# Attention and routing in front of a mixture of experts: logits from products of their own, and token reads carried into the routing

## The chip, the core and the metric

The kernel runs on one core of a Trainium2 chip. The metric is the device time of one execution in microseconds; of several runs the median is given. Engines are called TensorE (PE in the profile, its weight loads PEld), VectorE (DVE), ScalarE (ACT), GpSimd (POOL) and SyncE (SP, which only issues transfers here).

## What is computed

Cross attention between 512 tokens and 32 states for 8 batches and 8 heads of 64, in both directions; then all 576 rows of a batch go through a gate and one of 8 experts.

```
scores = 0.125 * x @ state.T;  a = softmax(scores);  xread = a @ state
scores2 = 0.125 * state @ x.T; a2 = softmax(scores2); sread = a2 @ x
x = concat([xread, sread], rows)            # 8 batches x 576 rows x 512
logits = x @ w_gate;  local = sigmoid(x @ w_local)
expert of row s: argmax(logits) if s == 0 or local < 0.5, else that of row s-1
out = softmax(logits)[expert] * (relu(x @ w1[expert]) @ w2[expert])
```

The choice of expert runs along the rows of a batch, so routing needs the logits of every row of the batch.

## The kernel before

The work has three stages: attention over eight batches, routing, experts. The tile framework is told to keep the order in which the program issues instructions (`manual_schedule`), so every engine's queue is the order of the calls in `Attention.run`, written out by hand: a loop over batches with three of them in flight, `now`, `then` and `later`.

One batch goes like this. `scores` multiplies states by tokens on TensorE: two banks of 128 x 512, one for each half `u` of the heads, partitions holding 4 heads x 32 states. From them:

- over tokens: maximum (`nb`, L387), exponential with its sum (`e2`, `z2`, L399), `turn` (four TensorE transposes each half, L445), a copy to SBUF (`turned_to`, L448), `state_reads` (L458), `states_to` (scaling by 1/z2, L464), a store to `rows` (L473).
- over states: a 32x32 block transpose on VectorE (`turned`, L410) brings tokens to the partitions, `over_states` takes the maximum over 32 states on VectorE (L417) and subtracts it on GpSimd (L418), `exponents` on ScalarE (L422), `shares` sums on VectorE (L426), adds 1e-9 (L427), inverts (L428) and multiplies on GpSimd (L429); `turn_back` (L435) turns the blocks back to `a`.

`token_reads(c)` then makes the result for 128 tokens: for each half one product of `a` with `sd`, which is 265 columns wide, 256 of states (block diagonal over heads) and 9 of states times gate weights. So the 9 logits (8 experts and the local gate) come out beside the values. The 530 columns are copied from PSUM (L485): by VectorE for c = 1 of all batches but the last, by ScalarE otherwise. GpSimd adds the two halves' 9 columns to `lt` (L507); for the last tokens VectorE does it straight from PSUM (L489, L490). One transfer stores 512 tokens of values to `rows` (L508). Logits of the states' rows come from `rt` (L470) by four small products (L500) and a copy (L502).

`rows` is a table in device memory from which the experts gather their tokens.

`Routing.route` is one chain. `choose` turns logits into an expert or "as before" (seven batches ahead of the last one, then the last). The choices are transposed on TensorE (`seq`, L611), a scan on VectorE runs along the rows (L620), products bring it back (`back`, L624), comparison gives `oh`, two products count (`tot`, `pre`, L637 and L638), and small VectorE and ScalarE steps make the first place of every expert, then a place for every row. `slots.expert` (L691) lets SyncE load the first weights; `two` (L763) lets GpSimd gather the first tokens. In gaps TensorE runs products whose result nobody reads (`keep`, L600): nine, five, twenty and eight of them.

The experts use nearly all of SBUF for weights; memory of attention and of the experts is opened one after the other. GpSimd clears `sd` and `lt` at the start. Attention uses 8 PSUM banks: two for scores, two shared (`t`), and two pairs for reads.

Of the kernel before, what the change touches and what calls it, by code (L numbers as in the profile page):

```python
# [50 lines left out]
def kernel(  # L51
# [31 lines left out]
    def banks(ctx, n):  # L83
        ps = ctx.enter_context(tc.tile_pool(name="ps", bufs=n, space=PSUM))
        return lambda parts=P, n=512, dt=F32: ps.tile([parts, n], dt, tag="ps", name="ps")

# [6 lines left out]
    lt = keep.tile([P, B, NC, E + 1], F32, name="lt")  # L93

# [5 lines left out]
    with ExitStack() as phase:  # L100
        make_identity(nc, ident)
        start = Attention(phase, tc, xn, xt, st, stt, wgl, wgs, lt, rows)
        route.constants(ident)
        nc.gpsimd.memset(lt, 0.0)
        start.diagonal(range(2))
        nc.gpsimd.memset(none, 0.0)
        nc.sync.dma_start(out=rows[NT:].rearrange("o q x -> o (q x)"), in_=none)
        start.run(route)
    with ExitStack() as phase:
        bank = banks(phase, 6)  # L110

        sums = phase.enter_context(tc.tile_pool(name="sums", bufs=1, space=PSUM))
        sums = [sums.tile([P, 512], F32, name=f"sum{i}") for i in range(2)]
        experts(phase, tc, bank, sums, w1, w2, rows, slots, route, route.route(bank, sums, lt, slots), out)
# [21 lines left out]
A = G * SC * 4  # L136


class Attention:


    def __init__(self, ctx, tc, xn, xt, st, stt, wgl, wgs, lt, rows):
        nc = self.nc = tc.nc
        self.xn, self.xt, self.lt, self.rows = xn, xt, lt, rows
        self.wg, self.wh = wgs[:, 0], wgs[:, 1]
        once = ctx.enter_context(tc.tile_pool(name="once", bufs=1))
        self.xp = ctx.enter_context(tc.tile_pool(name="xp", bufs=3))
        self.wk = ctx.enter_context(tc.tile_pool(name="wk", bufs=2))
        self.tp = ctx.enter_context(tc.tile_pool(name="tp", bufs=2))
        self.sm = ctx.enter_context(tc.tile_pool(name="sm", bufs=4))  # L150
        self.ps = ctx.enter_context(tc.tile_pool(name="aps", bufs=1, space=PSUM))
        self.vps = ctx.enter_context(tc.tile_pool(name="vps", bufs=2, space=PSUM))

# [5 lines left out]
        self.x_t = {0: self.load_t(0)}  # L159
# [4 lines left out]
        self.x_t[1] = self.load_t(1)  # L164
        self.x_n = {0: self.load_n(0)}


        self.sd = once.tile([P, B, G * VW], F32, name="sd")
        nc.gpsimd.memset(self.sd, 0.0)
# [7 lines left out]
    def diagonal(self, ks):  # L177
        nc = self.nc
        for k in ks:
            r = slice(32 * k, 32 * k + 32)  # L180
            to = self.sd[r, :, E + 1:E + 1 + D].rearrange("p b (g d) -> p b g d", g=G)
            nc.scalar.copy(to[:, :, :, DH * k:DH * k + DH],
                           self.states_of[r].rearrange("p (b g d) -> p b g d", b=B, g=G))

    def load_t(self, b):
        nc = self.nc
        xs = []
        for i in range(2):
            x_t = self.xp.tile([P, KT // 2, S], F32, name=f"x_t{i}")
            nc.sync.dma_start(out=x_t.rearrange("p k s -> p (k s)"), in_=self.xt[b][:, i * D * 2:(i + 1) * D * 2])  # L190
            xs.append(x_t)
        return xs

    def load_n(self, b):
        x_n = self.xp.tile([P, SC, G, KT, DH], F32, name="x_n")
        self.nc.sync.dma_start(out=x_n.rearrange("p c u k d -> p (c u k d)"), in_=self.xn[b])
        return x_n
# [4 lines left out]
    def bank(self, name, parts=P):  # L202
        return self.ps.tile([parts, 512], F32, name=name)

    def gates(self):
        nc = self.nc
        ws = [self.bank(f"t{u}") for u in range(G)]
        for u, w in enumerate(ws):
            r = slice(64 * u, 64 * u + 64)
            for b in range(B):  # L210
                for k in range(KT):
                    nc.tensor.matmul(w[32 * k:32 * k + 32, b * (E + 1):(b + 1) * (E + 1)],
                                     lhsT=self.states(b)[r, k, :], rhs=self.wh[r, k, :], start=True, stop=True)
        for u, w in enumerate(ws):
            nc.scalar.copy(self.sd[:, :, u * (E + 1 + D):u * D + (u + 1) * (E + 1)],
                           w[:, :B * (E + 1)].rearrange("p (b e) -> p b e", b=B))

    def keep(self, n):

        for i in range(n):  # L220
            self.nc.tensor.matmul(self.idle[:, 0, :], lhsT=self.zero[:, :P], rhs=self.zero, start=True, stop=True)

    def run(self, route):

        self.ident = route.ident
        self.idle = self.vps.tile([P, G, 512], F32, name="v")
        self.keep(10)
        now, then = Batch(self, 0), Batch(self, 1)
        now.scores()
        for b in (2, 3):  # L230
            self.x_t[b], self.x_n[b - 1] = self.load_t(b), self.load_n(b - 1)

        for u in range(G):
            now.turned(u)
            now.over_states(u)
        now.maximum(0)
        now.scaled(0)
        now.exponents(0)
        self.gates()
        now.exponents(1)  # L240
        now.exponents_over_tokens(0)
        now.shares(0)
        now.maximum(1)
        now.scaled(1, self.nc.vector)
        now.exponents_over_tokens(1)
        now.shares(1)
        self.keep(6)
        now.turn(0)
        self.diagonal([2, 3])
        then.scores()  # L250
        now.turn(1)
        now.turn_back(0)
        now.turn_back(1)
        for u in range(G):
            then.turned(u)
            then.over_states(u)
        now.token_reads(0)
        now.turned_to(0)
        now.turned_to(1)
        now.state_reads()  # L260

        later = Batch(self, 2)
        self.load(0)
        then.maxima()
        then.exponents(0)
        then.exponents(1)
        then.exponents_over_tokens(0)
        then.shares(0)
        then.exponents_over_tokens(1)
        then.shares(1)  # L270
        now.invert()
        now.token_reads(1)
        now.states_to()
        now.token_reads(2)
        now.states_to_rows()
        later.scores()
        then.invert()
        later.maxima()
        then.turn(0)
        then.turned_to(0)  # L280
        then.turn(1)
        now.token_reads(3)
        then.turned_to(1)
        then.turn_back()
        later.exponents_over_tokens(0)
        later.turned(1)
        later.exponents_over_tokens(1)
        later.turned(0)
        later.over_states()
        now.logits()  # L290
        later.invert()
        then.token_reads(0)

        for b in range(1, B):
            now, then, later = then, later, Batch(self, b + 2) if b + 2 < B else None
            if later:
                later.scores()
            now.state_reads()
            self.load(b)
            if b == B - 2:  # L300
                then.turn(0)
                then.turn(1)
            if 1 < b < B - 1:
                now.turn_back()
            if b == B - 2:
                for u in range(G):
                    then.exponents(u)
                    then.shares(u)
                    if u == 0:
                        now.states_to()  # L310
            elif then:
                then.exponents()
                now.states_to()
                later.maxima()
            else:
                now.states_to()
            if b > 1:
                now.token_reads(0)
            if later:
                then.shares()  # L320
            now.token_reads(1)
            now.states_to_rows()
            if b == B - 2:
                then.turn_back(0)
            if later:
                then.turn(0)
                then.turn(1)
                later.exponents_over_tokens(0)
            if then:
                then.turned_to(0)  # L330
            now.token_reads(2)
            if then:
                then.turned_to(1)
            if b == B - 2:
                then.turn_back(1)
            if later:

                later.turned(1)
                later.exponents_over_tokens(1)
                later.turned(0)  # L340
                for u in range(G) if b == B - 3 else (None,):
                    later.over_states(u)
            if b == B - 1:
                route.choose(self.lt, 0, b)
                now.state_logits()
                now.token_reads(3)
# [923 lines left out]
```

## Time and profile before

| | us |
|---|---|
| three runs | 559.71, 560.93, 562.62; median 560.93 |
| the profiled execution | 559.81 |
| its span, first to last instruction | 558.0 |
| granted TensorE clock, mean | 0.985 |

| stage | from to us | what ends it |
|---|---|---|
| attention | 0 to 84.3 | the last logits on VectorE |
| routing, first part | 84.3 to 95.25 | the number of the first expert |
| routing, second part | 95.25 to 111.75 | first product of the experts |
| experts | 111.75 to 558.0 | the end |

Busy time over the span: TensorE 529.5, VectorE 377.8, ScalarE 168.1, GpSimd 287.1 us. A line of instruction groups reads: line, engine, operation, output<-input, shapes, count | busy us, mean ns of one | idle time of the engine in front of them and what ended it. In the timeline each line begins with start and length in us; neighbouring instructions of one group are merged. In a table by stage each engine has its busy time and number of instructions.

### The profile page before, as it was taken

To read this page: it belongs to the slowest core of one execution; us is meant where nothing else is said; L and a number is where in the kernel's file an instruction comes from. 1 tells how busy PE (TensorE), PEld (TensorE's weight loads), DVE (VectorE), ACT (ScalarE), POOL (GpSimd) and SP (SyncE) were. 2 spreads that over 40 slices of the span, in tenths; PEclk is the share of its full clock that TensorE was granted. 3 is DMA by queue.
4 is the path that set the end of the run, shared out by engine and by line. 5 is a ranking of instruction groups with operands and counts; after the bars stand their busy time and mean duration, and the time that the engine had idled before them with its cause. 6 is when DMAs were issued, how large, how long until landed. Compare 5 with 4: busy or idle time off the path is not lost. (4 is left out here: it accounts for less than half of the span.)

```text
span 558.0 us, 12712 instructions
## 1 busy us (share of the span) xinstructions
PE 529.5 (95%) x4800; PEld 457.9 (82%) x4803; DVE 377.8 (68%) x625; ACT 168.1 (30%) x336; POOL 287.1 (51%) x366
## 2 busy tenths in 40 slices
PE   6879985999999999999999999999999999999994
PEld 2556662698989888898989898989899999989993
DVE  5879987673948474747565666665676766667674
ACT  4656651411132213231313122222232322223230
POOL 6444530165555555656464647463764546565454
PEclk9899997899999999999999999999999999999998
DMA  8999742689998989898979897966566575846652
GB/s 308 414 340 363 267 163 79 188 308 418 364 382 321 357 304 359 309 355 308 375 286 380 304 369 292 361 205 229 166 239 226 187 275 150 279 143 246 231 189 102
DMA packets 50793, 155.44 MB, mean 279 GB/s; under 512 B 9169, under 2 KB 9297, under 8 KB 47394
## 3 DMA queue, kind: packets, MB, share of 16 engines
q1 hardware_dynamic: 43202, 135.85, 66.6%
q0 software_dynamic: 7520, 18.69, 9.7%
q8 instruction: 40, 0.66, 0.5%
q14 instruction: 31, 0.25, 0.1%
HBM read 136.68 MB, written 17.89 MB: 277 GB/s over the span
## 5 line engine op out<-in xcount | busy, mean ns | idle before, releaser
L857 POOL DMA_INDIRECT xg<-rows,row x132 | 148.3, 1124 | 30.6 <-issue 30.1
L972 DVE TENSOR_TENSOR a<-a,a 128x1024 f32<-128x1024 f32 x64 | 76.8, 1220 | 21.1 <-DMA a<-in_w_dram 19.7
L1055 PE MATMUL ps<-xt,a 128*128 128x128 f32 x720 | 88.6, 276 | 0.0
L1055 PE MATMUL sum<-xs,a 128*128 128x128 f32 x720 | 87.8, 275 | 0.0
L1055 PEld LDWEIGHTS ps<-xt,a 128*128 128x128 f32 x720 | 84.4, 192 | 2.1 <-issue 1.8
L1055 PEld LDWEIGHTS sum<-xs,a 128*128 128x128 f32 x720 | 84.0, 192 | 0.0
L972 DVE TENSOR_TENSOR c<-c,c 128x1024 f32<-128x1024 f32 x64 | 75.4, 1219 | 3.0 <-DMA c<-in_w_dram 2.5
L1095 PE MATMUL ps<-c,h 128*128 128x256 f32 x312 | 74.7, 382 | 0.0
L1095 PEld LDWEIGHTS ps<-c,h 128*128 128x128 f32 x312 | 58.0, 190 | 10.9 <-issue 3.7
L1095 PE MATMUL ps<-c,hs 128*128 128x256 f32 x256 | 60.5, 379 | 0.0
L1038 POOL DMA_INDIRECT out_dram<-y,tok x32 | 34.5, 1079 | 43.6 <-DVE c L972 27.1
L1095 PEld LDWEIGHTS ps<-c,hs 128*128 128x128 f32 x256 | 48.6, 190 | 6.6
L1095 PE MATMUL sum<-c,h 128*128 128x256 f32 x200 | 47.2, 379 | 0.0
L972 DVE TENSOR_TENSOR h<-s,s 128x512 f32<-128x512 f32 x15 | 10.4, 692 | 54.2 <-ACT s L1078 54.2
L1095 PEld LDWEIGHTS sum<-c,h 128*128 128x128 f32 x200 | 38.0, 190 | 5.2
L871 POOL COPY tick<-s 1x1 f32<-1x1 f32 x45 | 16.3, 363 | 49.7 <-ACT s L1078 49.5
L482 PE MATMUL v<-sd,a 128*128 128x265 f32 x128 | 34.8, 406 | 4.7 <-DVE a L435 3.3
L1006 ACT COPY sum<-ps 128x256 f32<-128x256 f32 (+1 forms) x31 | 14.3, 460 | 71.0 <-PE ps L1055 49.5
L482 PEld LDWEIGHTS v<-sd,a 128*128 128x128 f32 x128 | 22.8, 193 | 12.0 <-DVE xr L485 3.5
L871 POOL COPY tick<-r 1x1 f32<-1x1 f32 x41 | 12.2, 299 | 36.6 <-ACT r L1100 34.3
L1100 ACT ACTIVATE r<-sum,prob 128x256 f32<-128x256 f32 x32 | 15.2, 475 | 51.7 <-PE sum L1095 49.2
L1095 PE MATMUL sum<-c,hs 128*128 128x256 f32 x128 | 30.2, 379 | 0.0
(228 smaller groups left out, 734.1 us busy)
## 6 DMA issues: line engine op xcount, KB each, us to landing
c<-in_w_dram SPq DMA_DIRECT2D x68, 512.0 KB, 7.8
a<-in_w_dram SPq DMA_DIRECT2D x64, 512.0 KB, 8.2
at<-in_w_dram SPq DMA_DIRECT2D x18, 1024.0 KB, 9.1
ct<-in_w_dram SPq DMA_DIRECT2D x18, 1024.0 KB, 7.8
x_t<-in_xt_dram SPq DMA_DIRECT2D x16, 512.0 KB, 7.9
x_n<-in_xn_dram SPq DMA_DIRECT2D x8, 1024.0 KB, 10.9
rows<-xr SPq DMA_DIRECT2D x8, 1024.0 KB, 4.2
xg<-rows,row POOLq DMA_INDIRECT x132, 5.2
```

What stands on the lines that cost most here:

```text
L482: nc.tensor.matmul(v[:, u, :VW], lhsT=self.a[:, u, c * P:c * P + P], rhs=at.sd[:, b, u * VW:(u + 1) * VW], start=True, stop=True)
L857: nc.gpsimd.indirect_dma_start(out=to.rearrange("p k t -> p (k t)"), out_offset=None, in_=rows.rearrange("n q x -> (n q) x"), in_offset=ba ...
L871: nc.gpsimd.tensor_copy(tick, value)
L972: nc.vector.tensor_tensor(out, a, b, op=op)
L1006: nc.scalar.copy(y, x)
L1038: nc.gpsimd.indirect_dma_start(out=out, out_offset=to, in_=y, in_offset=None, bounds_check=NT - 1, oob_is_err=False)
L1055: nc.tensor.matmul(to[:, m * P:m * P + P], lhsT=w[:, j, m * P:m * P + P], rhs=x[:, j, :], start=begin and m == 0 and j == 0, stop=(m == FK ...
L1095: nc.tensor.matmul(to, lhsT=x[:, m, :], rhs=w[:, m, :], start=begin and m == 0, stop=(m == FK // 2 - 1), skip_group_check=True)
L1100: nc.scalar.activation(to, t, Act.Copy, scale=p)
```

## The change

The change does five things.

1. Logits of tokens get products of their own. `gl` holds states times gates, 32 columns for each half and batch (9 used); `logits` multiplies `gl` by `a`, four column groups of 32 and 128 tokens each, both halves added in PSUM, and VectorE turns the 128x128 result into `lt`, which is now 32 wide. `sd` keeps the values alone, 256 columns for each half. The adds of L489, L490 and L507 go.
2. All reads are copied by ScalarE.
3. Ten of the 32 token reads are issued after the last logits, inside `route`: `reads(n)` goes on with the list of steps up to and including the n-th read. They stand where three of the `keep` groups stood: two and three reads around the transposes of the choices, one ahead of the counts, the rest behind them. `keep(20)` becomes `keep(14)`.
4. The order of attention is a table of steps, `STEPS`, two letters and the batch (and half or quarter): `sc` scores, `tr` turned, `mo` and `sb` maximum and subtraction, `ex` exponents, `zh` halves, `zs` sums, `zi` inverses, `ml` shares, `tb` turn_back, `vv` and `xr` a read and its copy, `wr` the store, `lg` and `lt` logits. Exponentials over states are handled by half `u`; scores have four PSUM banks, all else shares four. `choose` for seven batches stands where `ch0` is.
5. From the second batch on GpSimd adds the exponentials of states 0 to 15 to those of 16 to 31 (`halves`), and VectorE sums 16 instead of 32 values.

Besides, the constants of the routing are made before attention starts, the memsets come in the order `gl`, `lt`, `sd`, `none`, and memory is laid out so that values still waiting (`a`, `sd`, `xr`, `lt`) lie on the other side of SBUF from the first weights, with the rest of the experts' memory opened after the first part of the routing.

```diff
-        start.diagonal(range(2))
-        nc.gpsimd.memset(none, 0.0)
-        nc.sync.dma_start(out=rows[NT:].rearrange("o q x -> o (q x)"), in_=none)
-        start.run(route)
...
+            route.constants(ident)
+            start.clear()
+            route.more_constants()
+            start.run(route)
+        bank = Banks(tc, 4)
+        routing = route.route(bank, lt, slots, start.reads)
...
+STEPS = """
+sc0 xt11 xt10 tr00 ga sd1 mo00 xt20 tr01 sd0 sb00 mx01 xt30 gl mx00 ex00 sc1 mo01 nb0 sd2 xt21 zs00 sb01 et01
...
+mo21 zh11 ec11 zs10 sb21 vv02 zs11 zi1 sr1 xr02 mx20 ml10 xt40 mx21 ex21 vv00 ml11 tb10 st1 vv01 xt41 mo20 xr00
...
+xr42 vv43 sk6 et71 zs70 zi7 lg6 xr43 iv7 tu71 ml70 lt6 vv40 ch0 ec71 ml71 sr7 xr40 tb70 wr4 vv53 tb71 st7 lg7
+rt7 xr53 sl7 lt7 vv51 sk7 ch1 ws7 vv52 xr51 vv50 xr52 vv70 xr50 vv61 wr5 xr70 vv63 xr61 vv62 xr63 vv60 xr62 vv73
+xr60 vv72 wr6 xr73 vv71 xr72 xr71 wr7
+"""
...
+        self.wk = ctx.enter_context(tc.tile_pool(name="wk", bufs=4))
...
+        self.sp = ctx.enter_context(tc.tile_pool(name="sp", bufs=4, space=PSUM))
...
+    def reads(self, n):
+
+        def going():
+            nonlocal n
+            n -= self.steps[0][0] == "vv"
+            return n >= 0
+        self.more(going)
...
+    def halves(self, b, u):
+
+        e1, h = self.get("e1", b, u), self.new(self.wk, "zh", (b, u), [P, A, N // 2], bufs=2)
+        self.nc.gpsimd.tensor_tensor(h, e1[:, :, :N // 2], e1[:, :, N // 2:], op=Alu.add)
...
+    def logits(self, b):
+
+        l = self.of["l", b] = self.bank(n=P)
         for u in range(G):
...
+            a = self.get("a", b, u).rearrange("p (i q t) -> p q i t", i=SC, q=Q)
+            for q in range(Q):
+                self.nc.tensor.matmul(l[SQ * q:SQ * q + SQ, :], lhsT=self.gl[:, b, u, :], rhs=a[:, q],
+                                      start=(u == 0), stop=(u == G - 1))
+
+    def logits_turned(self, b):
+        self.nc.vector.transpose(self.lt[:, b, :SC, :].rearrange("p i e -> p (i e)"), self.get("l", b))
+
+    def token_reads(self, b, c):
+        v = self.of["v", b, c] = self.bank()
+        for u in range(G):
+            d = slice(u * GD, u * GD + GD)
+            self.nc.tensor.matmul(v[:, d], lhsT=self.get("a", b, u)[:, c * P:c * P + P], rhs=self.sd[:, b, d],
+                                  start=True, stop=True)
+
+    def reads_kept(self, b, c):
+        xr = self.new(self.late, "xr", (b,), [P, SC, D], bufs=3)
+        self.nc.scalar.copy(xr[:, c], self.get("v", b, c))
...
-        keep(9)
+        reads(2)
...
-        keep(5)
+        reads(3)
...
+        reads(1)
...
+        reads(NB)
...
-        keep(20)
+        keep(14)
```

## The prediction

> **What bounds the kernel now.** I read the page's slices first, then busy time by stage with stage borders taken from the timeline, then one batch's groups, the waits, and the routing's timeline.
>
> ```profile
> PE   6879985999999999999999999999999999999994
> DVE  5879987673948474747565666665676766667674
> PEclk9899997899999999999999999999999999999998
> ```
>
> A slice is 13.95 us. From the ninth on TensorE is full: that is the expert stage. The change touches only the first eight slices.
>
> ```profile
> 63.04:71.20 8.16, 7.64 (x168) 5.97 (x162) 7.56 (x16) 5.37 (x12) 4.62 (x5) 1.00 0.40 142
> 71.20:84.30 13.10, 10.83 (x120) 7.79 (x119) 10.87 (x43) 7.34 (x15) 4.54 (x7) 1.00 0.49 172
> 84.30:95.25 10.95, 5.06 (x31) 2.25 (x33) 8.57 (x36) 1.11 (x5) 0.00 (x0) 0.79 0.25 97
> 95.25:111.75 16.50, 15.55 (x119) 9.43 (x119) 11.17 (x30) 6.20 (x15) 2.27 (x3) 0.83 0.59 160
> 111.75:558.00 446.25, 438.36 (x3612) 400.44 (x3612) 289.18 (x407) 108.89 (x208) 243.97 (x314) 1.00 0.78 282
> ```
>
> Columns: stretch, length, busy time per engine, granted clock, DMA share, GB/s. The rows are one attention batch (8.16 us), the end of attention, routing up to the expert number, routing up to the first expert product, and the experts. The experts run TensorE at 438.36 of 446.25 us, so what is won or lost ahead of them goes through one for one. In a batch VectorE (7.56) and TensorE (7.64) are both nearly full; DMA is not (0.40).
>
> ```profile
> L482 PE MATMUL v<-sd,a 128*128 128x265 f32 x16 | 4.3, 398 | 0.5 <-DVE a L435 0.4
> L435 DVE STREAM_TRANSPOSE a<-e 128x1024 f32<-128x1024 f32 x1 | 1.2, 1223 | 0.0
> L426 DVE TENSOR_REDUCE z<-e 128x32 f32<-128x1024 f32 x1 | 1.2, 1220 | 0.5 <-ACT e L422 0.5
> L485 DVE COPY xr<-v 128x530 f32<-128x530 f32 x1 | 0.6, 648 | 0.0
> ```
>
> VectorE's only idle time in that batch is 0.5 us ahead of the sums (L426): VectorE sets the pace, and the token reads (L482) are more than half of TensorE's work.
>
> ```profile
> 84.39 2.12 PE L600 MATMUL sum<-place,identb 128*128 128x512 bf16 x8 [1.09 <-DVE lt L584]
> 85.29 0.17 DVE L590 SCALAR_TENSOR_TENSOR top<-lt,own 128x5 bf16<-128x5 f32 x1
> 86.44 0.39 PE L611 MATMUL ps<-identb,top 128*8 128x128 bf16 x4
> 88.77 0.25 PE L624 MATMUL ps<-identb,run 8*128 8x8 bf16 x4 [0.65 <-DVE run L620]
> 90.13 0.30 PE L638 MATMUL ps<-oh,before 128*128 128x320 bf16 x1
> 93.60 0.21 ACT L673 ACTIVATE behind<-end 128x8 f32<-128x8 f32 x1
> 94.18 0.15 ACT L679 COPY end<-ps 8x2 f32<-8x2 f32 x1 [0.29 <-PE ps L677]
> 95.25 0.15 ACT L691 CAST expert<-ps 1x1 int32<-1x1 f32 x1 [0.92 <-PE ps L690]
> ```
>
> Routing is one serial chain, VectorE with short TensorE and ScalarE steps between. TensorE's gaps there are what the moved reads fill.
>
> **The change part by part.** T is the end of the last logits on VectorE: 84.24 us now (after the copy and add of L489 and L490).
>
> VectorE, over the eight batches. Gone: seven copies of reads, 7 x 0.65 = 4.6. Sums over halves: rows L426 give 0.654 for 512 elements and 1.22 for 1024, so 1.1 ns an element and about 0.09 fixed; 256 elements are an estimated 0.37. Seven batches x (1.22 - 0.74) = 3.4 gone. Constants (78.07 to 79.97) move ahead: 1.9 gone from here. The last batch's copy and add, 0.3. Added: eight transposes of logits, 128x128, at 0.29 (row L470, same size) = 2.3; two 512-wide instructions where one 1024-wide stood, 1.28 against 1.15 from start to start, twice in five or six batches, 1.4. Net -6.5. Busy time from the first transpose (8.17) to T is 67.3 now (stage rows), so 60.8 after: packed, T would be 69.0.
>
> What is not packed. Now 76.1 us hold 67.3 busy, 8.8 idle: 4.1 before 38.5 us, 2.4 in four batches, 2.2 at the end. After: (a) front. The table starts two batches before the first is done, and scores get four banks instead of two; I keep 1.5 (bounds 0.5 and 4.1). The constants now stand ahead of the first transpose; a cast of 128 elements took 0.619 (L534) beside a GpSimd memset, against 0.186 for L568's copy, so the longer memsets (gl, and lt 32 wide: about 1.5 us more, at 0.86 ns an element from sd's 3.63 us) can hold them. Bounds 0 and 1.5, I take 0.6. GpSimd itself ends its memsets at about 7.7, ahead of its first subtraction (9.69 now). (b) in the batches: the sums now wait for GpSimd's halves behind ScalarE's exponentials; behind a waiting sum stand other batches' transposes and maxima on VectorE, and for those GpSimd's subtractions. Between sum and halves the table puts other batches' work, and hands exponentials on in halves, so I take half of the present 2.4, 1.2 (bounds 0 and rival 2). (c) the end: the last values, then 0.6 for logits on TensorE, 0.5 idle. (d) the shared port.
>
> Port. The row first, of the groups by shape in the first 115 us:
>
> ```profile
> L427 DVE TENSOR_SCALAR z<-z 128x16 f32<-128x16 f32 x6 | 2.0, 332 | 0.2
> L427 DVE TENSOR_SCALAR z<-z 128x32 f32<-128x32 f32 x5 | 0.9, 181 | 0.2
> ```
>
> The smaller form takes longer: two of its six took 0.65, both beside a GpSimd multiply. The Trainium skill (SBUF — State Buffer, Who interferes with whom) says why: a VectorE scalar operation on SBUF in two-port mode and a GpSimd operation exclude each other for a whole instruction. That speaks against this change: GpSimd gets 14 more additions, and busy goes from 4.25 to about 5.6 in each batch (two 512-wide halves of 1.05 twice, two additions at about 0.62 from rows L418 and L429, 0.2 of scaling). By the row (2 of 6 by 0.47) about 16 such operations cost 2.5; by the rule (busy 0.75, half a GpSimd instruction each) 6; with a kind order, 0. I take 2.8, near the row.
>
> The choices now read logits 32 apart instead of 9: same counts, no row shows a stride; 0 (up to 0.4).
>
> T after: 69.0 + 1.5 + 0.6 + 1.2 + 0.5 + 2.8 = 75.6, less than now by 8.6.
>
> TensorE up to T: reads 22 of 32 instead of 32, at 256 instead of 265 columns: 0.98 instead of 1.02 each. Without reads a batch is 3.6 (scores 1.1, transposes 1.05, state reads 1.06, state logits 0.42). New logits: 16 passes of 128 columns in four column groups. State reads, 64 passes of 64 columns, take 1.06, so half the work is an estimated 0.5. 8 x 4.1 + 1.3 (gates) + 22 x 0.98 = 55.7 from 5.9 us: ends at 62, up to 70 with early gaps. It has 5 us of cover under T, and would set T if its gaps grew beyond that. ScalarE copies 22 reads before T where it copies 25 now, though it takes over all 32. Inputs: x_t of the third batch is 4.8 MB into the stream; at the 405 GB/s of that stage it is in at about 14.5 us, when VectorE still works on the second. Nothing. GpSimd's small logit add (0.26 a batch) goes.
>
> Routing. Ten reads (9.8 us) and their copies are strewn through it, in place of 9 + 5 + 6 warming products. Times from T; in brackets now.
> - TensorE after state logits does three reads (2.94), one of them queued ahead; the turned choices start at about 2.85 (2.2, held by nine warming products while top was there at 1.2). +0.65.
> - Then three reads, 2.94, where VectorE needs only 1.8 for hold and scan: the products back (L624) start at 6.3 (4.5). +1.1.
> - One read ahead of the counts: those end at 8.05 (6.2). +0.1.
> - Four reads behind the counts, 3.9, where TensorE idled 3.2; their copies stand in front of less, behind, number and end8 on ScalarE. The last copy ends at about 12.7; behind at 13.1 (9.6). VectorE waits for behind, then end8, and all of its chain behind them: +1.35. Expert number at 14.2 (11.0).
> Sum +3.2; bounds +1 (copies that keep up with TensorE) and +4.5 (each copy late by one).
>
> SP: three more rows stores stand in front of the first weights. The last is issued at about T + 12.8, before the expert number is known, and lands about 4.2 later (rows<-xr) at T + 17; the first gather from rows starts at T + 21.3 + 3.2. Cover 7 us, nothing. Weights: their 16 issues alone take 8.85 us, the last lands 3.7 ahead of the first product. Nothing. Fewer warming products (14 for 20): TensorE waits there for VectorE's inp anyway (101.6). Nothing, or up to 2 if the clock falls.
>
> Sum: -8.6 + 3.2 = -5.4. The profiled execution's own time is 559.81 (span 558.0 and 1.8 around it), 1.1 below the median of 560.93; a difference carries over: 560.9 - 5.4 = 555.5.
>
> **The rivals.**
> 1. The order runs nearly packed: 69.0 + 1.5 + 0.5 and 1.0 at the port is T at 72.0, routing +2.5: -9.7, 551.2. For: both full engines get a lead of a batch. Against: the port.
> 2. The order written in the table does not fit the chip: VectorE stands behind a chain of subtraction, exponential, halves, sum, inverse, product (1.05 + 0.63 + 0.62 + 0.37 + 0.45 + 1.05 = 4.2) that crosses engines five times; 0.5 us more waiting per batch takes 4 more: -1.4, 559.5. For: L426 waited 3.5 us for exponentials now. Against: 4.2 is below a batch's 7.2.
> 3. Slower: the clock.
>
> ```profile
> 90.00:91.00 1.00, 0.43 (x2) 0.79 0.02 8
> 91.00:92.00 1.00, 0.00 (x0) 0.50 0.00 0
> ```
>
> It fell to half 2.7 us after the fifth warming product had ended, with TensorE at 0.35 and 0.13 in between, and stayed there until 100.6. The Trainium skill (TensorE: Matmul & The Clock Gate, Why this matters for your kernels) warns of idle gaps above about 3 us, the trace shows one a little shorter. Reads at half clock take 1.96, so the eleven in the chain would add up to 10.8: -5.4 + 10.8, 566.3. It decides from six slow reads on. By the rule the reads themselves keep the clock: 1.0, and nothing added. I side with that. That the change does nothing is out: the built order has ten reads behind the last logits.
>
> **How the numbers follow.** A measurement of this kernel can tell about 0.5%, 2.8 us. Forecast 0.55 (own range 552.5 to 558.5), rival 1 0.22, rival 2 0.15, rival 3 0.08. Faster by over 0.5%: nearly all of the first and all of the second, 0.75; within 0.16; slower 0.09. Range 550.3 to 560.5: below it a T under 71, above it rival 3 and the bad end of rival 2.
>
> **What would show it.** Right: T at 74 to 79, VectorE near 7.3 us a batch, sums at 0.37, expert number T + 13 to 15, clock 1.0 in routing, experts again 446. Wrong: T above 82 with VectorE waits for GpSimd (rival 2), half clock beside reads (rival 3), T above 77 with TensorE full.

## The result, and the profile after

The changed kernel takes 556.14 us (median; 554.26 to 557.22), the kernel before 559.71 beside it on the same chip: a ratio of 0.9932 (0.9911 to 0.9953), 3.6 to 3.8 us less. The profiled executions are 555.67 us (span 553.7) and 559.81 (span 558.0).

First the changed kernel in 40 slices, as shown of before:

```profile
PE   6898996999999999999999999999999999999993
DVE  8999878572866574848474747566677766767663
PEclk8899999799999999999999999999999999999998
```

VectorE is fuller in the first four slices (8999 for 5879; one is 13.84 us), and the clock's notch behind attention has moved from the seventh slice to the eighth. The time is in the stages. These rows are attention from 37.8 us on, the routing up to the expert number, from there to the first expert product, and the experts; columns as before (stretch, length, busy time of PE, PEld, DVE, ACT and POOL, granted clock, DMA share, GB/s):

```profile
37.80:75.70 37.90, 33.97 (x636) 24.28 (x625) 34.43 (x89) 26.29 (x62) 25.23 (x31) 1.00 0.70 250
75.70:88.50 12.80, 11.26 (x62) 8.79 (x62) 8.53 (x36) 7.04 (x16) 0.00 (x0) 1.00 0.68 243
88.50:106.70 18.20, 13.56 (x115) 8.67 (x114) 11.18 (x30) 6.19 (x15) 2.13 (x2) 0.81 0.71 199
106.70:553.70 447.00, 438.36 (x3612) 400.48 (x3612) 289.17 (x407) 108.73 (x208) 242.66 (x314) 1.00 0.79 282
```

Attention ends at T = 75.71. Before, its last instruction was this one:

```profile
84.17 0.16 DVE L490 TENSOR_TENSOR lt<-lt,v 128x9 f32<-128x9 f32 x1
```

It ends at 84.33 (the prediction's 84.24 is 0.09 short of that), so T is 8.6 us earlier. The routing takes 12.8 instead of 10.9: +1.9. The stretch up to the first expert product takes 18.2 instead of 16.5: +1.7. The experts take 447.0 instead of 446.25, with TensorE's busy time the same to the hundredth (438.36): the +0.7 is behind its last product. The sum is -4.3, as in the spans: half of what attention won was given back on the way.

VectorE's groups by shape up to T, in the changed kernel (line, operation, out<-in, count, busy us, mean ns, idle before):

```profile
L345 DVE TENSOR_REDUCE z<-zh 128x16 f32<-128x256 f32 x14 | 5.4, 395 | 0.0
L453 DVE CAST iof<-io 128x128 f32<-128x128 int32 x1 | 5.3, 5350 | 0.4 <-POOL io L446 0.4
L316 DVE TENSOR_SCALAR z<-z 128x2 f32<-128x2 f32 x8 | 3.6, 450 | 0.0
L350 DVE TENSOR_SCALAR z<-z 128x32 f32<-128x32 f32 x7 | 2.6, 367 | 0.2
```

The sums over halves take 395 ns and never wait. The additions of 1e-9 are tiny, yet one on two elements a partition takes 450 ns in the mean; the shortest of the eight takes 100. A cast of 128 elements takes 5.35 us. The longest of the eight shows what it stood behind:

```profile
49.38 0.89 DVE L316 TENSOR_SCALAR z<-z 128x2 f32<-128x2 f32 x1
49.19 1.05 POOL L332 TENSOR_TENSOR e<-e,m 128x512 f32<-128x512 f32 x1
```

It ends at 50.27, just behind GpSimd's subtraction at 50.24; the one before it, at 48.51, ends in the same way with GpSimd's multiply. These are costs of GpSimd at work beside VectorE, and they come back below.

The routing in the timeline of the changed kernel (start, us, engine, line), from the last values of attention to the expert number:

```profile
75.59 0.12 DVE L403 COPY lt<-p 32x9 f32<-32x9 f32 x1
78.22 0.39 PE L534 MATMUL ps<-identb,top 128*8 128x128 bf16 x4
81.44 0.25 PE L547 MATMUL ps<-identb,run 8*128 8x8 bf16 x4
82.83 0.30 PE L562 MATMUL ps<-oh,before 128*128 128x320 bf16 x1
87.21 0.20 ACT L598 ACTIVATE behind<-end 128x8 f32<-128x8 f32 x1
88.54 0.15 ACT L616 CAST expert<-ps 1x1 int32<-1x1 f32 x1 [1.00 <-PE ps L615]
```

From T these are 2.5, 5.7, 7.1, 11.5 and 12.8 us; before they were 2.1, 4.4, 5.8, 9.3 and 10.9. The delay is 0.4, 1.3, 1.3, 2.2 and 1.9. It grows by 0.9 at two places: at the products back (L547), which have three reads ahead of them on TensorE, and at `behind`, which has the copies of the last four ahead of it on ScalarE. The single read adds nothing. And the part behind the expert number:

```profile
88.44 3.20 PE L524 MATMUL ps<-place,identb 128*128 128x512 bf16 x14
95.05 0.42 PE L682 MATMUL ps<-bf,inp 128*128 128x4 bf16 x8 [3.42 <-DVE inp L676]
97.36 3.57 PE L524 MATMUL sum<-place,identb 128*128 128x512 bf16 x8
100.73 3.89 PE L682 MATMUL ps<-pb,inp 128*128 128x98 bf16 x40
106.73 14.56 PE L1070 MATMUL ps<-xt,a 128*128 128x128 f32 x128
```

Fourteen warming products take 0.23 us each, so they end at 91.64; then TensorE has nothing for 3.4 us. Eight more from 97.36 take 0.45 each: the clock is at a half. Two one-us stretches of TensorE alone (length, busy, granted clock, DMA share, GB/s) show the gap and the half clock behind it:

```profile
94.00:95.00 1.00, 0.00 (x0) 1.00 0.87 242
97.00:98.00 1.00, 1.00 (x18) 0.50 0.96 209
```

### The profile page after: what moved, and what is told of

It is laid out like the page before. It is cut to its first block, busy times and chain, and to the rows that moved or that the text cites. A ratio compares the mean times of both kernels' runs of the same rounds, so it can differ in the third digit from the quotient of the medians.

```text
span 553.7 us, 12962 instructions
## 1 busy us (share of the span) xinstructions
PE 527.3 (95%) x4905; PEld 458.7 (83%) x4905; DVE 378.7 (68%) x635; ACT 172.4 (31%) x348; POOL 296.3 (54%) x383
## 5 line engine op out<-in xcount | busy, mean ns | idle before, releaser
L1026 PEld LDWEIGHTS ps<-c,h 128*128 128x128 f32 x312 | 58.0, 190 | 10.9 <-issue 3.7
L421 PE MATMUL p<-sd,a 128*128 128x256 f32 x128 | 32.0, 391 | 0.0
L986 PE MATMUL ps<-xs,a 128*128 128x128 f32 x240 | 29.3, 275 | 0.0
```

The costliest lines, as they stand in the source:

```text
L421: self.nc.tensor.matmul(v[:, d], lhsT=self.get("a", b, u)[:, c * P:c * P + P], rhs=self.sd[:, b, d], start=True, stop=True)
L986: nc.tensor.matmul(to[:, m * P:m * P + P], lhsT=w[:, j, m * P:m * P + P], rhs=x[:, j, :], start=begin and m == 0 and j == 0, stop=(m == FK ...
L1026: nc.tensor.matmul(to, lhsT=x[:, m, :], rhs=w[:, m, :], start=begin and m == 0, stop=(m == FK // 2 - 1), skip_group_check=True)
```

## The experiments

The kernels ran in three sets, each beside the kernel before on one chip (its medians there: 559.57, 560.77 and 558.31 us), so ratios are to be compared, not times. The first set is keep28, nokeep8, readsfirst and spread, the second nohalves, before_halves, noadds and joined, the third the rest. T, the expert number and the first expert product are from each kernel's one profiled execution.

| kernel | ratio (95%) | T | expert number | first expert product | span |
|---|---|---|---|---|---|
| before | 1 | 84.33 | 95.25 | 111.75 | 558.0 |
| changed | 0.9932 (0.9911 to 0.9953) | 75.71 | 88.54 | 106.73 | 553.7 |
| keep28 | 0.9898 (0.9875 to 0.9920) | 76.20 | 89.02 | 105.57 | 552.7 |
| nokeep8 (output wrong) | 0.9909 (0.9882 to 0.9937) | 76.13 | 88.95 | 105.54 | 551.5 |
| readsfirst | 1.0020 (1.0008 to 1.0032) | 84.19 | 94.80 | 111.36 | 557.3 |
| spread | 0.9947 (0.9928 to 0.9965) | 76.39 | 86.44 | 106.89 | 555.2 |
| nohalves | 0.9968 (0.9951 to 0.9985) | 78.84 | 91.54 | 109.56 | 557.5 |
| before_halves | 1.0135 (1.0113 to 1.0157) | 92.85 | 103.78 | 120.69 | 568.8 |
| noadds | 0.9942 (0.9923 to 0.9961) | 75.20 | 88.03 | 106.23 | 555.0 |
| joined | 0.9921 (0.9900 to 0.9941) | 76.16 | 88.98 | 107.06 | 554.7 |
| ys4 | 0.9936 (0.9915 to 0.9958) | 78.88 | 91.70 | 109.92 | 556.1 |
| ys4_adds | 0.9922 (0.9897 to 0.9946) | 76.34 | 89.16 | 107.35 | 553.5 |
| all_four | 0.9907 (0.9886 to 0.9927) | 77.23 | 90.06 | 108.09 | 554.3 |

**readsfirst: what moving the reads is worth.** The changed kernel with all ten late reads ahead of the last logits again, and warming products in the routing as before.

```diff
-        self.more(lambda: self.steps[0] != ("ch", [1]))
-        self.steps.pop(0)
+        at = self.steps.index(("ch", [1]))
+        late = self.steps[at + 1:]
+        cut = self.steps.index(("lg", [7]))
+        moved = [("xr", [5, 3]), ("vv", [5, 1])]
+        self.steps = (self.steps[:cut] + moved + [s for s in late if s[0] != "ws"]
+                      + [s for s in self.steps[cut:at] if s not in moved] + [s for s in late if s[0] == "ws"])
+        self.more(lambda: True)
...
-        reads(2)
+        keep(9)
...
-        reads(3)
+        keep(5)
...
-        reads(1)
...
-        reads(NB)
...
-        keep(14)
+        keep(20)
```

> The changed kernel with all reads ahead of the last logits and the 9, 5 and 20 warming products of before in the routing: the move of ten reads undone, all else kept. Theory: T goes from 75.7 to 85.5 (ten reads at 0.98 in front of the last logits on TensorE), the expert number comes 11.0 behind T as before (12.9 now), second part 16.5: expert product at 113 against 106.7, span about 560, 559 to 562 median. So the move alone is worth 4 to 6 us and all the rest of the change about nothing at the end of attention. Rival: TensorE has room ahead of T (34.0 busy in 37.9 us) and VectorE sets T: T at 80 to 82, median 555 to 558.

T is 84.19, about where it stood before the change, and the time is 0.2% above before. VectorE's timeline in readsfirst shows why:

```profile
74.58 0.27 DVE L393 STREAM_TRANSPOSE rt<-ys 128x128 f32<-128x128 f32 x1
83.83 0.32 DVE L420 STREAM_TRANSPOSE lt<-p 128x128 f32<-128x128 f32 x1 [8.99 <-PE p L416]
```

VectorE has nothing left at 74.85 and waits 9.0 us for TensorE's last logits. TensorE works 67.6 of the 75.0 us from the first transpose to T, so another place for the reads in attention could have won back less than the 7.4 us in which it idles, not the 8.6; such an order was not run. With the reads in attention TensorE's stream ends it, and the relief of VectorE buys nothing. In the routing they cost 2.2 (12.8 for 10.6 from T), and 1.6 behind it. What moving them is worth in the end is the difference of the ratios, 0.0088, or 4.9 us.

**nohalves and before_halves: what the halves on GpSimd are worth.** In the first the changed kernel sums over all 32 states on VectorE again; in the second the kernel before gets the halves alone, for its batches from the second on.

```diff
     def halves(self, b, u):
 
-        e1, h = self.get("e1", b, u), self.new(self.wk, "zh", (b, u), [P, A, N // 2], bufs=2)
-        self.nc.gpsimd.tensor_tensor(h, e1[:, :, :N // 2], e1[:, :, N // 2:], op=Alu.add)
+        return
```

> The changed kernel without GpSimd's additions of halves: VectorE sums 32 exponentials again, in the same places of the table. Theory: 14 sums of 0.65 instead of 0.395 add 3.6 us of busy VectorE time; GpSimd has 10.2 us less to do, so that VectorE's small additions (L316, 0.450 mean where 0.105 is its own length, L350, 0.367 where 0.18 is) stand less behind GpSimd, 1 to 1.5 us back. T later by 2 to 3 us, median 558.5. Rival: what the halves save they cost again at the shared port and in waiting for GpSimd: T the same, 556.

```diff
+        add = e1
+        if self.b:
+            add = self.at.wk.tile([P, A, N // 2], F32, name="zh")[:, self.half(u)]
+            nc.gpsimd.tensor_tensor(add, e1[:, :, :N // 2], e1[:, :, N // 2:], op=Alu.add)
-        nc.vector.tensor_reduce(z1.rearrange("p a o -> p (a o)"), e1, axis=AX, op=Alu.add)
+        nc.vector.tensor_reduce(z1.rearrange("p a o -> p (a o)"), add, axis=AX, op=Alu.add)
```

> The kernel before with nothing but the halves: from the second batch on GpSimd adds states 0 to 15 to 16 to 31 and VectorE sums 16. Theory: in the hand-written order nothing stands between exponentials and sums, so VectorE waits for GpSimd about 1.0 us (512 elements at 1.05) in each batch, while a sum of 512 instead of 1024 elements gives 0.57 back: 0.4 us a batch slower, T later by 2 to 3, 562. The halves pay only with the table's order. Rival: the sum's wait is hidden by the wait for exponentials that is there already, T earlier by up to 3, 557.

Without the halves T is 78.84, 3.1 later, near the 3.4 that the prediction took off for them (some of it may be the clock, at a half from about 48.5 to 52 us in this execution; keep28 had that too). By the ratios (0.9968 against 0.9932, their intervals just touching) they are worth 2.0 us of time. One part of the expectation failed: the small additions were to get back 1 to 1.5 us with GpSimd's 10.2 us of halves gone, and they stayed as long as they were:

```profile
L316 DVE TENSOR_SCALAR z<-z 128x2 f32<-128x2 f32 x8 | 3.6, 454 | 0.0
L349 DVE TENSOR_SCALAR z<-z 128x32 f32<-128x32 f32 x7 | 2.5, 357 | 0.2
```

Put into the old order they cost 7.6 us (568.40 against 560.77), far more than either theory had it. The waits of VectorE in before_halves (line <- what it waited for: us in all, times, longest), and one batch of it in the timeline:

```profile
DVE z L430 <- POOL zh L429: 14.6, 9, 1.9
```

```profile
67.60 1.92 POOL L418 TENSOR_TENSOR e<-e,m 128x1024 f32<-128x1024 f32 x1 [1.24 <-DVE lt L506]
70.69 1.29 POOL L429 TENSOR_TENSOR zh<-e 128x512 f32<-128x512 f32 x1 [0.21 <-ACT e L422]
72.01 0.69 DVE L430 TENSOR_REDUCE z<-zh 128x32 f32<-128x512 f32 x1 [1.84 <-POOL zh L429]
```

Subtraction, exponential, halves and sum follow each other, and VectorE stands for 1.84 in front of the sum, where it saved 0.53 (0.69 for 1.22): this is the second rival, on a kernel where it can happen. In the changed kernel the same wait is 0.0 (row L345 above), since other batches' steps stand between. The new order is what makes the halves pay.

**keep28 and nokeep8: the 1.7 us behind the expert number.** The first fills TensorE's gap with 28 warming products for 14. The second leaves the clock alone and leaves out the eight warming products that stand ahead of the last 40 small ones; its output is wrong without them, for a reason that stays open, so only its times up to the first expert product are read, and not its ratio.

```diff
-        keep(14)
+        keep(28)
```

> The changed kernel with 28 instead of 14 warming products behind the expert number. Theory: the second part of the routing (18.2 us against 16.5 before the change) is longer because TensorE stands idle from 91.6 to 95.05 and its clock falls to 0.50 from 96.3 on, so that the next eight warming products take 3.6 us and hold the products behind them. 28 products of 0.23 us fill the gap up to 94.9: clock 1.00 throughout, second part 16.5, 1.7 us less, 554.4. Rival, the second part is longer because the first weights and the last rows stores share the transfers: second part stays at 18.2, no change.

```diff
         yield
-        keep(8)
         nc.vector.tensor_tensor(bc[:, 0], inb, over(cols), op=Alu.mult)
```

> The changed kernel without the eight warming products behind the first tokens' places. Theory: at half clock it is these products, standing in TensorE's queue, that cost, not the products behind them (40 of them took 3.9 us at full clock before the change and 3.9 at half clock after it). Then these start at 99.0, when VectorE's pb is ready, instead of 100.7: 1.0 to 1.7 us less, 554.8. Rival: the slow clock costs wherever it is, and now lasts into the experts: second part 17.5 to 18.2 and the first expert products slower, 0 to 1 us less, or more time.

The same two stretches of TensorE in keep28:

```profile
94.00:95.00 1.00, 1.00 (x6) 1.00 0.89 197
97.00:98.00 1.00, 0.79 (x22) 1.00 1.05 215
```

In its profiled execution the clock stays whole, the eight products take 1.67 instead of 3.57, and the stretch from the expert number to the first expert product is 16.55 for 18.2. In nokeep8 the clock is at a half from 97 to 103, and the stretch is 16.6 all the same. The eight and the 40 products in keep28, then the 40 in nokeep8:

```profile
98.04 1.67 PE L524 MATMUL sum<-place,identb 128*128 128x512 bf16 x7
99.59 3.87 PE L682 MATMUL ps<-pb,inp 128*128 128x98 bf16 x40
99.54 3.88 PE L682 MATMUL ps<-pb,inp 128*128 128x98 bf16 x40 [1.63 <-DVE pb L694]
```

(One of keep28's eight has no record.) Together they name the way of the loss: the 40 small products take 3.87 at full clock (keep28) and 3.88 at half (nokeep8), so the clock doesn't matter to them; what it stretches is the eight products queued ahead of them on TensorE. keep28 has the lowest ratio, 0.9898, but its interval overlaps those of the changed kernel, joined, ys4, ys4_adds and all_four.

Its gain isn't safe either: in joined and all_four (below), also with 28 products, the clock fell at about 97.6 and 99.1, and the eight took 3.07 and 3.43. Here are joined's stretches:

```profile
97.00:98.00 1.00, 0.76 (x20) 0.79 1.05 232
98.00:99.00 1.00, 0.82 (x2) 0.50 0.99 242
```

TensorE had been as busy ahead of that as in keep28. In spread (next) it fell as well, at 94.8, with no wait of TensorE above 0.74 us. So the gap isn't needed for the clock to fall; whether it was the cause in the changed kernel, and what else decides it, stays open.

**spread: fewer reads inside the routing.** The reads stand as 0, 2, 1 and 3 in the routing's four places, and the last four, with ten warming products, behind the expert number.

```diff
-        reads(2)
         seq = bank(B, T, BF16)
...
-        reads(3)
+        reads(2)
         back = bank(P, NC * B, BF16)
...
-        reads(NB)
+        reads(3)
...
-        keep(14)
+        reads(NB)
+        keep(10)
```

> The changed kernel with the ten reads placed otherwise: none ahead of the choices' transposes (2 now), two instead of three behind them, one, three instead of four behind the counts, and the last four behind the expert number with ten warming products instead of 14. Theory: the chain waited for TensorE and ScalarE three times (1.5, 1.0 and 0.7 us of VectorE idle), and TensorE idled 3.4 us later; so the expert number comes at T + 11.2 (12.9 now), the clock stays at 1.00, second part 16.5 to 17: 2.5 to 3.5 us less, 553. Rival: the last stores now stand in front of the first weights on SyncE and hold them by 3 us: the second part grows by 2 to 3 and nothing is left.

The routing is even quicker than before the change, T + 10.05 for T + 10.9, so the reads in it do cost time. But all of it is lost: the first expert product starts at 106.89, and the clock fell here too (0.50 from 95 to 98). In the timeline of spread the last reads' copies and their stores, the weights and the gather:

```profile
90.09 0.59 ACT L426 COPY xr<-p 128x512 f32<-128x512 f32 x1 [0.28 <-PE p L421]
92.30 9.57 SPq L844 DMA_DIRECT2D a<-in_w_dram  x16
98.34 0.95 POOL L794 DMA_INDIRECT y<-rows,two  x1 [0.30 <-issue]
105.98 1.11 PE L824 MATMUL ps<-ident,y 128*128 128x128 f32 x4 [1.16 <-DMA y<-rows,two]
```

The weights' 16 issues begin only at 92.30, behind the last store on SP, and TensorE waits 2.3 us for the gathered rows, which land 7.4 us after the gather instead of 4.7. The expert number is not the only thing that the experts wait for: the last rows' stores and the weights stand in one queue on SP, and the weights' issue begins 5.9 us behind the expert number here (92.30 for 86.44), where in the changed kernel it begins 1.8 behind it (90.33 for 88.54). The rival of the queue came true: the stretch is 20.45 for 18.2. That the late weights are what slows the gather was not tested by itself.

**noadds, ys4, ys4_adds: is the shared port on the path?** noadds leaves out the two additions of 1e-9 (L316 and L350), so that the sums are inverted as they are. ys4 adds two more buffers for `ys`; ys4_adds has those alone.

```diff
-        nc.vector.tensor_scalar(z2, z2, 1e-9, None, Alu.add)
         nc.vector.reciprocal(z2, z2)
...
-        self.nc.vector.tensor_scalar(z1, z1, 1e-9, None, Alu.add)
         self.nc.vector.reciprocal(z1, z1)
```

> The changed kernel without the additions of 1e-9 to the two sums of exponentials (each sum is at least 1, so that the addition changes no bit). It leaves out just the 17 VectorE operations that stood behind GpSimd at the shared port: 6.9 us of VectorE time in the profile, of which about 2.4 are their own and 4.5 blocking. Theory (port): T earlier by 4 to 6, at 70 to 72, median 551.5. Rival (only their own length counts, the blocked time is taken from idle time anyway): T earlier by 2 to 2.5, 554. Rival (TensorE, busy 34.0 of 37.9, now sets T): T at 72.5 to 73.5, VectorE with new waits for TensorE.

VectorE's busy time from the first transpose to T falls from 62.0 to 55.5, as it should. T falls by 0.5, and the ratio, 0.9942, is that of the changed kernel within its interval. VectorE's waits of noadds in attention:

```profile
DVE rt L386 <- ACT ys L382: 4.1, 3, 1.7
DVE lt L413 <- PE p L409: 3.1, 4, 1.3
DVE a L357 <- POOL e L353: 1.7, 3, 1.2
```

In the changed kernel the first is absent, the second 1.8, the third 1.2. The clock differs too. These rows are from the first transpose to T in the changed kernel, noadds and joined (below, also without the additions); columns as in the stages:

```profile
9.20:75.70 66.50, 58.20 (x1093) 39.11 (x1094) 62.04 (x146) 47.72 (x107) 44.74 (x54) 0.95 0.82 308
9.20:75.20 66.00, 60.31 (x1093) 39.82 (x1094) 55.47 (x129) 47.25 (x107) 44.43 (x54) 0.90 0.83 310
8.40:76.16 67.76, 57.71 (x1093) 38.99 (x1094) 55.57 (x127) 48.02 (x107) 44.47 (x54) 0.97 0.82 306
```

So noadds alone proves little, since TensorE worked 2.1 us longer at its lower clock. But joined had the clock at 0.97 and the same relief of VectorE, and its T is 76.16: the relief isn't hidden by the clock. ScalarE in turn waited 5.8 us for the stores that still read the two buffers of `ys`, so I took those for the floor.

```diff
-        ys = self.new(self.tp, "ys", (b,), [P, G, DH])
+        ys = self.new(self.tp, "ys", (b,), [P, G, DH], bufs=4)
```

> The kernel without the two additions of 1e-9 (noadds), and four buffers instead of two for `ys`, the states' values that ScalarE copies out of PSUM and SP stores. In noadds VectorE waited 4.1 us for the copies into ys, and ScalarE 5.8 us for the stores that still read the old ys. Theory (the additions of 1e-9 did sit on VectorE's path, and the stores' buffers were the floor just beneath it): without that wait T, the end of the last logits on VectorE, falls from noadds' 75.2 to 71 to 72, and the time by 3 to 4 us against noadds: a ratio near 0.988. Rival (the floor is TensorE's stream or the round from GpSimd to ScalarE and back): the wait moves to the products or to GpSimd, T stays at 74.5 to 75.2, the ratio near 0.994.

> The changed kernel, additions of 1e-9 included, with four buffers for `ys` alone. VectorE never waits for ys there, so by the theory T stays within 0.5 us of 75.7 and the time at a ratio near 0.993; by the rival that ScalarE's 5.4 us of waiting for the stores is what delays the whole chain, T falls by 2 or more and the ratio to 0.990 or less.

That theory fell. ys4's ratio is 0.9936, again the same, and its waits are in other places:

```profile
DVE lt L413 <- PE p L409: 3.5, 4, 1.4
DVE lt L401 <- PE p L397: 3.3, 1, 3.3
DVE rt L386 <- ACT ys L382: 1.5, 1, 1.5
```

VectorE now waits 6.8 us for TensorE's logits, and TensorE in turn waits 5.6 for input x_t (2.5 in the changed kernel). In this execution, the longest of its six (558.07), the clock was at a half from 50 to 60 us as well. ys4_adds does as little as its theory said. So the port's price is in VectorE's busy time but hardly in the end of attention: with it gone, VectorE waits for others instead. Whether TensorE or its inputs then end last, and whether the clock's dips come from VectorE's new pace or by themselves (the changed kernel had one from 11.0 to 17.9 but none there, keep28 one from 48.5 to 51.9), isn't settled.

**joined and all_four.** joined is keep28 and noadds with three casts of the front (iof, iob, identb) on ScalarE, the first of which is shown; all_four adds the four buffers of ys.

```diff
-        nc.vector.tensor_copy(iof, io)
+        nc.scalar.copy(iof, io)
...
```

> The changed kernel with 28 warming products, without the additions of 1e-9, and with three of the constants' casts (iof, iob, identb) on ScalarE, where GpSimd's memsets can't hold them (on VectorE two of them stood 5.3 us). If the three theories add up: first transpose at 8.2 instead of 9.2, T 1 us earlier than without the additions alone, and 1.7 us from the clock: 549. Rival: the front is set by the inputs (scores of the second batch wait for x_t until 12.4), the casts give nothing: 550.

> Everything together: no additions of 1e-9, four buffers for `ys`, the first casts on ScalarE, 28 warming products instead of 14 behind the routing. If the floor was the stores' buffers, T is near 71.5, and with the clock kept the first expert product starts near 101: about 549 us, a ratio of 0.980. If it wasn't, T stays near 75.5 and the time near 555. In the joined kernel the clock fell to a half at 97.8 us in spite of the 28 products, where in keep28 it did not; if it falls here as well, 1.5 us of that is gone, and the number of warming products is not what decides it.

Neither beats keep28. The casts take 0.28 each on ScalarE, but VectorE doesn't come free: its timeline in joined, with GpSimd's large memset, reads

```profile
1.82 5.03 DVE L467 CAST cols<-ci 128x40 bf16<-128x40 int32 x1
2.97 4.42 DVE L475 TENSOR_SCALAR ev<-iof 128x8 f32<-128x8 f32 x1
3.31 3.50 POOL L212 MEMSET sd<- 128x4096 f32 x1
```

The next instructions in line take the wait in the casts' place: L467 ends at 6.85, just behind this memset (6.81), and L475 at 7.39, just behind the next one (7.36). The first transpose starts at 8.40 instead of 9.20, and T doesn't follow (76.16).

## Why the prediction was right, point by point

- **T: 75.6 predicted, 75.71.** That it fits to 0.1 is luck; its terms were off in both directions. Start of the first transpose: 9.20, where 8.17 + 0.6 was taken; the casts beside the memsets cost 1.0, within the bound of 1.5. Busy time: 60.8 + 2.8 at the port predicted, 62.0 measured. Idle time: 4.5 of 66.5, for 1.5 + 1.2 + 0.5. The errors, +0.4, -1.6 and +1.3, cancel. The busy time is the smaller because records overlap: summed singly, VectorE's instructions go from 73.1 to 69.0 us, -4.1 where -6.5 + 2.8 was predicted, and they overlap by 7.0 instead of 5.7. Single terms fit: the sums over halves 0.395 for an estimated 0.37, the additions on GpSimd 735 ns for 0.62, the instructions split in two 21.4 us instead of 20.1 (transposes and maxima of the exponentials).
- **The port: 2.8 predicted, about 3.5.** L316, L350 and L510 take about 5 us beyond their undisturbed durations (0.10, 0.18 and 0.45 each), where the same ones took about 1.6 before. The Trainium skill's rule (SBUF — State Buffer, Who interferes with whom) is borne out in kind: an addition on VectorE ended just behind GpSimd's instruction. The reason given, that GpSimd gets 14 more additions, is not: without them (nohalves) the same additions take as long, and with them in the old order (before_halves) they take no longer than before. That leaves the new order, in which more of them fall beside a GpSimd instruction; this is argued from these two runs, not tested by itself.
- **TensorE's cover: 5 us predicted, none measured.** TensorE was to be through at 62, or at 70 with early gaps. From 5.9 us to the last logits at 75.35 it was busy for 60.0 us, where 55.7 was summed, and idle for 9.5; its clock was at a half from 11.0 to 17.9. VectorE waited 0.35 for it at the end. The number of T came out although this term did not.
- **The reads' move as the cause: shown** by readsfirst. The prediction summed T as VectorE's list; the runs add that without the moved reads T doesn't fall at all, and with VectorE relieved further it doesn't fall either. VectorE and TensorE are nearly equally late, and the sum by one engine held because the change relieved both. What logits of their own, ScalarE's copies or the new order give by themselves was not run.
- **Routing: +3.2 predicted, +1.9.** Each of its steps was a little too dear: the choices' transposes start at T + 2.5 (2.85 predicted), those back at 5.7 (6.3), the counts at 7.1 (8.05). The largest part is the last one: ScalarE's copies keep up with the reads, 585 ns each behind a read of 0.95, so `behind` comes at 11.5, not 13.1. That was the prediction's own lower bound. The expert number at T + 12.8 is just outside the 13 to 15 that it gave as a sign of being right.
- **Fewer warming products: "nothing, or up to 2 if the clock falls".** The second came, +1.7, and was not in the sum. Before, 20 products at half clock filled 7.3 us:

```profile
95.15 7.27 PE L600 MATMUL sum<-place,identb 128*128 128x512 bf16 x20
```

In the changed kernel 14 at full clock fill 3.2, TensorE has nothing for 3.4, and the clock falls 1.3 us after that gap. This fits the rule of the Trainium skill (TensorE: Matmul & The Clock Gate, Why this matters for your kernels) that gaps above about 3 us lose the clock, which the prediction used for the reads alone. But spread, joined and all_four lost the clock here without such a gap, so the rule doesn't tell when it falls, and that this gap was the cause isn't shown.
- **SP and the weights: nothing. Right** for the changed kernel, whose TensorE waits ahead of the experts for no DMA; spread shows the cover gone once the reads go behind the expert number.
- **Clock in the reads: 1.0 predicted, 1.00** in the routing's row. The third rival didn't come.
- **Experts the same: right** in TensorE's time; +0.7 lies behind its last product, where the last store is issued 0.7 later.
- **Sum: -5.4 predicted, -4.3 in the profiled executions.** The routing was taken 1.3 too dear, the stretch behind it and the end 2.4 too cheap; these errors cancel in part.

## What to carry to other kernels

When two engines are nearly equally late, work has to leave both: here the relief of VectorE without TensorE's bought nothing (readsfirst), and a further relief of VectorE alone hardly moved T (noadds, joined); the relief of TensorE alone was not run. A stage that fills another engine's gaps should be costed for what it displaces, and filler whose only job is the clock is to be counted in microseconds at the clock that it will then have, not in instructions. Moving an operation to another engine pays where the order puts other work between it and its user: the same halves were worth 2.0 us in the one order and cost 7.6 in the other.

## What the hardware showed that I had not expected

- VectorE can be held by GpSimd through several instructions: behind three memsets without a gap, a cast of 128 elements took 5.35 us (0.28 on ScalarE), and moving it away handed the wait to the next ones, 5.03 and 4.42 us.
- Half clock can last long under full load: from 96.4 to 103.2 us in the changed kernel, with TensorE busy for 6.62 of these 6.8 us.
- Forty bf16 products of 98 columns with a weight load each take the same at half clock as at full: 3.88 us (nokeep8) and 3.87 (keep28).
